# Causal attention in fp32: one score layout for all pairs of heads, whole loads of q and k, and fewer bytes moved

## Chip, cores and metric

One core of a Trainium2 chip. The metric is the device time of one execution in microseconds (us); a smaller time is better. The time is the median of several runs, beside one execution that the hardware profiler recorded.

## The reference

```python
scores = (q @ k.T) / sqrt(64), causal mask            # q, k, v: 4 batches x 12 heads x 448 x 64
attn   = softmax(scores);  x = attn @ v               # then x as 4 x 448 x 768
u = x + (relu(x.T @ w_tok1) @ w_tok2).T               # mixing of tokens, 448 -> 256 -> 448
x = u + relu(u @ w_ch1) @ w_ch2                       # feed-forward, 768 -> 1536 -> 768
theta = x @ w_theta
u = x + w_tok_r @ (x * cos(theta)) + w_tok_i @ (x * sin(theta))
out = u + relu(u @ w_ch)
```

All inputs are fp32 but the weights, which come as 64-bit numbers and are rounded on the chip.

## The kernel before, in words

The 48 heads (4 batches x 12) are worked in 24 pairs, numbered 0 to 23 (in words, pair one is number 0). A pair's two heads lie side by side along the free dimension: q and k are tiles of 64 partitions (the head dimension) by 896 columns. A pair's scores are made in seven tiles (`TILES`, line 326): tile 0 holds the first 64 query rows of both heads, tiles (i, h) with i = 1, 2, 3 hold 128 query rows of head h against 64 + 128 i keys. `scores` (line 338) makes a tile: the matmul (lines 358, 360), the masked maximum on VectorE (line 367), the exponential with its sum on ScalarE (line 369), and then the turning of the probabilities, so that `pv` (line 397) can multiply them with the values.

There are three kinds of pairs. Pairs 0 to 11 (`NATIVE`) multiply q and k as fp32; their tiles of q and k have 128 partitions of which the upper 64 are cleared by memset (line 281: VectorE for pair 0, POOL for pairs 1 to 11) while a DMA fills the lower 64 (line 286). Pairs 12 to 23 load q and k twice over, in both halves of the partitions (lines 288 and 290), and split them into a high and a low part (lines 297 to 302). Pairs 0 to 7 (`NATPV`) also multiply probabilities and values as fp32: every tile has a buffer of its own out of three, TensorE transposes it block by block (line 376, 1 + i blocks of 128 x 128, where the first block of a tile with i > 0 is half zeros: 64 cleared columns stand ahead of the buffer, line 257), ScalarE copies the blocks out of PSUM (line 378) into one of five buffers, and line 407 multiplies them with the values, 128 columns wide but for the last tile. Pairs 8 to 23 lay both heads of a tile side by side, the blocks of the first in reverse order, so that the two half blocks meet in the middle and make one; they split the probabilities into two fp16 parts (lines 387, 388), turn them by a DMA transpose on the SP queue (line 391), and multiply in three passes (lines 416, 424). Their values are split too, by ScalarE (line 124), POOL (line 163) and VectorE (line 323). The values have nine blocks of 64 columns.

The order of the work is written as 168 steps, one per tile (`steps`, line 620). Each step emits a tile's scores; `late_steps` (line 630) emits `pv` of the tile four steps earlier (five for pairs 8 to 23); at a pair's first step the loads of the next pair are emitted (line 695). Between these lie the rounding of the weights (`ROUNDINGS`, line 39: fetch on SP, line 173; ScalarE line 177, POOL line 130, VectorE lines 185 and 186; scaled split, POOL line 163 and VectorE line 197; store on SP, line 581) and, from step 53 on, the units of the feed-forward network (`UNIT_STEPS`): 24 units per batch, each of 18 fp16 matmuls of 448 columns (lines 231 to 233), whose weights `load_unit` (line 531) reloads from memory. The frame that builds the program then orders each engine's instructions by priorities and by its own estimate of times, so the order on an engine is not the order of the text; an engine works its list strictly in order. SP issues nearly all DMAs, so a wait on SP holds back all that stands behind it.

After the attention follow the remaining units, and the last layer (lines 724 on), which the change doesn't touch.

Of the kernel before, what the change touches and what calls it, by code (L numbers as in the profile page):

```python
# [18 lines left out]
P = 128  # L19
# [9 lines left out]
BUFS = dict(ut=12, h2=8, acc=12, ws=8, wf=3, raw=3, sb=3, pt=5, t=3, junk=1)  # L29
# [5 lines left out]
LATE_CONVERT = 16  # L35
FIRST_UNIT, DENSE, RATE = 53, 88, (42, 29)
# [18 lines left out]
def fused(ctx, tc, q, k, v, w_tok1, w_tok2, w_ch1, w_ch2, w_theta, w_tok, w_ch, out):  # L55
# [42 lines left out]
    def mm_bank():  # L98
        return bank("mm", 4)
# [154 lines left out]
    sb_all = ac.tile([P, BUFS["sb"] * 512], F32, tag="sb", name="sb")  # L254
    sbufs = [sb_all[:, j * 512:(j + 1) * 512] for j in range(BUFS["sb"])]
    for sb in sbufs:
        nc.gpsimd.memset(sb[:, 0:64], 0.0)
    pt_all = ac.tile([P, BUFS["pt"] * 512], F32, tag="pt", name="pt")
    ptfs = [pt_all[:, j * 512:(j + 1) * 512].rearrange("p (n q) -> p n q", q=P) for j in range(BUFS["pt"])]
    blocks = pt_all.bitcast(F16).rearrange("p (n q) -> p n q", q=P)  # L260
    count = [0]
# [14 lines left out]
    def prep(b, pr):  # L276
        qr = ap2.tile([P, 2 * S], F32, tag="qk_raw", name="q_raw", bufs=2)
        if b * NPR + pr in NATIVE:
            kr = ap2.tile([P, 2 * S], F32, tag="kh", name="k_pad")
            for t, src in ((kr, k), (qr, q)):  # L280
                (nc.vector if b * NPR + pr == 0 else nc.gpsimd).memset(t[64:128], 0.0)
                if b * NPR + pr == 0 and t is qr:
                    for c in (slice(0, 2 * P), slice(2 * P, 2 * S)):
                        nc.scalar.dma_start(out=t[0:64, c], in_=src[b, pr, 0:64, c])
                else:
                    loads[b * NPR + pr] = nc.sync.dma_start(out=t[0:64], in_=src[b, pr, 0:64])
        else:
            loads[b * NPR + pr] = nc.sync.dma_start(out=qr, in_=q[b, pr])
            kr = ap2.tile([P, 2 * S], F32, tag="qk_raw", name="k_raw", bufs=2)
            nc.sync.dma_start(out=kr, in_=k[b, pr])  # L290
        vr = ap2.tile([P, 9 * D], F32, tag="v_raw", name="v_raw")
# [3 lines left out]
        else:  # L295
            qs = ap2.tile([P, 2 * S], F32R, tag="qs", name="qs")
            copy_to(pick("qhi"), qs, qr)
            rest_to(pick("qlo"), qs[64:128], qr[64:128], qs[64:128])
# [15 lines left out]
    def value_split(n):  # L314
# [5 lines left out]
        hi = ap2.tile([P, 9 * D], F16, tag="v_hi", name="v_hi", bufs=2)  # L320
# [17 lines left out]
    def scores(pp, i, h):  # L338
# [6 lines left out]
        if pp.native_pv:  # L345
            cut = lambda t: t[:, h * S:h * S + n]
            if i == 0:
                cut = lambda t: t.rearrange("p (h s) -> p h s", h=2)[:, :, 0:64]
            msk = mask[:, S - kk:S]
        else:  # L350
            c0 = S if h == 1 else S - n + (64 + (n - kk) // 2 if i == 0 else 0)
            cut = lambda t: t[:, c0:c0 + n]
            if h == 0:
                src = ps[:, (n - kk) // (2 if i == 0 else 1):][:, 0:kk]
            msk = mask[:, S - kk:S] if h == 1 else mask[:, S - P:S - P + kk]
        if i == 0:
            msk = mask0.rearrange("p a b -> p (a b)")
        nc.tensor.matmul(ps[:, 0:n], lhsT=lhs, rhs=cut(pp.kh), start=True, stop=pp.kl is None)  # L358
        if pp.kl is not None:
            nc.tensor.matmul(ps[:, 0:n], lhsT=lhs, rhs=cut(pp.kl), start=False, stop=True)  # L360
        if pp.native_pv:
            full = sbufs[count[0] % BUFS["sb"]]
            sb = full[:, 64:64 + kk]
        else:
            both = (sb_all[:, 0:640], sb_all[:, 640:1536])[i % 2][:, 0:P if i == 0 else 2 * kk]
            sb = both[:, h * kk:(h + 1) * kk]
# [27 lines left out]
    def twice(ap):  # L394
        return ap.unsqueeze(1).to_broadcast([P, 2, D])
# [630 lines left out]
```

## Time and profile before

| | |
|---|---|
| median of 3 runs | 872.34 us (870.3 to 873.48) |
| the profiled execution | 871.68 us |
| its span, from the first to the last instruction | 869.9 us |
| mean granted TensorE clock | 0.998 of full speed |
| TensorE busy | 839.3 us (96%), 5699 matmuls |
| weight loads busy | 532.7 us (61%) |
| VectorE, ScalarE, POOL busy | 598.9, 531.3, 265.6 us |
| DMA | 151.99 MB |

PE is TensorE's matmul side, PEld its weight loads, DVE is VectorE, ACT is ScalarE, POOL is GpSimd, SP the engine that issues DMAs; a q behind a name (SPq) is the engine's sequencer. L376 is line 376 of the kernel. The ends of matmuls are modelled and they overlap, so a busy PE can still have room. A row of a group gives its count, its busy time in us and the mean duration in ns, and behind the bar the idle time of the engine before it, with what ended it.

### The profile page before, as it was taken

The numbers are of one execution on the slowest core, as the hardware profiler recorded it, in microseconds if no ns is written. First come the engines' busy times: TensorE is split into PE (matmuls) and PEld (weight loads), VectorE is DVE, ScalarE is ACT, GpSimd is POOL, SyncE is SP. The second block draws the span as 40 slices with busy tenths as digits, with TensorE's granted clock in tenths as the row PEclk, the third lists the DMA queues.
The fourth block names the chain that finished last, engine by engine and source line by source line (L and its number), as shares of the span: only waits on it lengthen the run. The fifth ranks groups of instructions, "written<-read, shape, count | busy, mean of one in ns | idle before, by whom it ended". The sixth has DMA issues, their size and how long they took to land.

```text
span 869.9 us, 16014 instructions
## 1 busy us (share of the span) xinstructions
PE 839.3 (96%) x5699; PEld 532.7 (61%) x5699; DVE 598.9 (69%) x1294; ACT 531.3 (61%) x1223; POOL 265.6 (31%) x445
## 2 busy tenths in 40 slices
PE   7999998899899999999999999999999999999997
PEld 6988856565657566576756655565555555555554
DVE  6788787999988556567774367669747548567541
ACT  6798786777767637367653276547647447456441
POOL 4366564547662220413222035331111001101000
PEclk9999999999999999999999999999999999999999
DMA  6866869999999976856475597702613123131012
GB/s 217 258 208 201 269 198 271 261 310 294 289 255 313 280 226 140 233 132 125 141 173 203 186 278 265 227 30 73 197 40 108 40 90 98 40 119 58 25 45 75
DMA packets 121024, 151.99 MB, mean 175 GB/s; under 512 B 76848, under 2 KB 88048, under 8 KB 120944
## 3 DMA queue, kind: packets, MB, share of 16 engines
q1 hardware_dynamic: 120400, 149.95, 59.4%
q0 software_dynamic: 384, 0.79, 0.4%
q8 instruction: 45, 0.74, 0.3%
q10 hardware_dynamic: 160, 0.23, 0.1%
q14 instruction: 35, 0.29, 0.1%
HBM read 110.56 MB, written 22.81 MB: 153 GB/s over the span
## 4 chain that ended last, share of the span: by engine, by line
PE 67%; DMA 10%; DVE 8%; ACT 5%; issue 5%; POOL 5%; SPq 0%; ACTq 0%; POOLq 0%; DVEq 0%
PE ps_mm L232 15%; PE ps_mm L231 15%; PE ps_mm L233 15%; DMA pt<-ph 5%; PE ps_sc L358 3%; PE ps_sc L231 3%; PE ps_sc L232 3%; PE ps_sc L233 3%; PE ps_pv L407 2%; DMA raw_w<-in_w_theta_dram 1%; PE ps_pv L424 1%; ACT junk L124 1%; ACT sb L369 1%; DVE sb L367 1%; PE ps_mm L376 1%
## 5 line engine op out<-in xcount | busy, mean ns | idle before, releaser
L231 PE MATMUL ps_mm<-h,ws 128*128 128x448 f16 x432 | 151.7, 354 | 1.6 <-DVE g L140 1.0
L232 PE MATMUL ps_mm<-h,ws 128*128 128x448 f16 x432 | 152.7, 354 | 0.1
L233 PE MATMUL ps_mm<-h,ws 128*128 128x448 f16 x432 | 152.5, 354 | 0.0
L231 PEld LDWEIGHTS <-ws 128*128 128x128 f16 x720 | 70.5, 98 | 67.2 <-issue 5.3
L233 PEld LDWEIGHTS <-ws 128*128 128x128 f16 x720 | 70.5, 98 | 63.9 <-issue 3.7
L232 PEld LDWEIGHTS <-ws 128*128 128x128 f16 x720 | 70.5, 98 | 62.5 <-issue 5.2
L369 ACT ACTIVATE sb<-sb,mx 128x320 f32<-128x320 f32 (+3 forms) x168 | 89.1, 533 | 25.6 <-DVE mx L367 25.0
L231 PE MATMUL ps_mm<-ut,ws 128*128 128x448 f16 x288 | 101.1, 353 | 1.4 <-DMA rawt<-x2d 1.3
L232 PE MATMUL ps_mm<-ut,ws 128*128 128x448 f16 x288 | 101.5, 353 | 0.8 <-DVE ut L197 0.8
L233 PE MATMUL ps_mm<-ut,ws 128*128 128x448 f16 x288 | 101.6, 353 | 0.0
L367 DVE CUSTOM_DVE_ANT_0 sb<-ps_sc,mask 128x320 f32<-128x320 f32 (+3 forms) x168 | 73.4, 455 | 17.7 <-PE ps_mm L376 11.3
L124 ACT ACTIVATE junk<-acc 128x448 bf16<-128x448 f32 x72 | 41.2, 572 | 59.1 <-DVE acc L912 41.3
L358 PE MATMUL ps_sc<-k_pad,q_raw 128*128 128x192 f32 (+3 forms) x168 | 56.9, 441 | 9.1 <-DMA k_pad<-in_k_dram 4.3
L787 POOL TENSOR_SCALAR tmp<-tmp 128x384 f32<-128x384 f32 x28 | 15.6, 556 | 148.6 <-ACT tmp L786 145.6
L388 DVE SCALAR_TENSOR_TENSOR ph<-sb,ph 128x128 f16<-128x128 f32 (+1 forms) x64 | 46.8, 736 | 19.0 <-ACT ph L160 18.3
L163 POOL TENSOR_SCALAR h<-t 128x448 f16<-128x448 f32 x48 | 35.2, 735 | 75.7 <-ACT t L497 75.2
L497 ACT ACTIVATE t<-ps_mm,c_scale 128x448 f32<-128x448 f32 x48 | 30.0, 625 | 41.3 <-PE ps_mm L233 36.2
L160 ACT ACTIVATE ph<-sb 128x128 f16<-128x128 f32 (+1 forms) x64 | 39.6, 625 | 25.6 <-DMA pt<-ph 25.3
L499 DVE TENSOR_TENSOR h<-t,h 128x448 f16<-128x448 f32 x48 | 32.0, 670 | 27.0 <-POOL h L163 26.9
L130 POOL TENSOR_SCALAR raw<-raw 128x768 f32<-128x768 f32 (+2 forms) x34 | 35.4, 1041 | 41.6 <-ACT wf L177 37.0
L231 PE MATMUL ps_sc<-th,ut 128*128 128x384 f16 x144 | 46.9, 326 | 0.0
L233 PE MATMUL ps_sc<-th,ut 128*128 128x384 f16 x144 | 46.8, 326 | 0.0
(218 smaller groups left out, 2119.4 us busy)
## 6 DMA issues: line engine op xcount, KB each, us to landing
ws<-w_c SPq DMA_DIRECT2D x120, 384.0 KB, 4.6
raw<-in_w_ch_dram SPq DMA_DIRECT2D x30, 768.0 KB, 5.6
w_c<-ws SPq DMA_DIRECT2D x30, 384.0 KB, 4.3
v_raw<-in_v_dram SPq DMA_DIRECT2D x24, 288.0 KB, 4.9
q_raw<-in_q_dram SPq DMA_DIRECT2D x12, 448.0 KB, 4.2
k_raw<-in_k_dram SPq DMA_DIRECT2D x12, 448.0 KB, 5.4
x2d<-acc SPq DMA_DIRECT2D x24, 224.0 KB, 3.8
acc<-x2d SPq DMA_DIRECT2D x24, 224.0 KB, 2.6
```

The source lines that it names most:

```text
L124: nc.scalar.activation(j[:, 0:src.shape[-1]], src, AF.Square, accum_out=dst)
L130: nc.gpsimd.tensor_scalar(out=dst, in0=a, scalar1=b, scalar2=c, op0=ALU.mult, op1=ALU.mult)
L160: nc.scalar.activation(dst, src, AF.Copy, scale=scale)
L163: e.tensor_scalar(out=dst, in0=src, scalar1=scale, scalar2=0.0, op0=ALU.mult, op1=ALU.add)
L231: nc.tensor.matmul(ps, lhsT=ka(a[:, 0]), rhs=kb(b[:, 0]), start=first, stop=False)
L232: nc.tensor.matmul(ps, lhsT=ka(a[:, 0]), rhs=kb(b[:, 1]), start=False, stop=False)
L233: return nc.tensor.matmul(ps, lhsT=ka(a[:, 1]), rhs=kb(b[:, 0]), start=False, stop=last)
L358: nc.tensor.matmul(ps[:, 0:n], lhsT=lhs, rhs=cut(pp.kh), start=True, stop=pp.kl is None)
L367: pp.first = nc.vector.tensor_tensor_reduce(out=sb, in0=src, in1=msk, op0=ALU.add, op1=ALU.min, scale=-0.125, scalar=3.0e38, accum_out=pp. ...
L369: pp.last = nc.scalar.activation(sb, sb, AF.Exp, bias=pp.mx[:, j:j + 1], scale=-1.0, accum_out=pp.sm[:, 2 + j:3 + j])
L388: nc.vector.scalar_tensor_tensor(out=lo, in0=both, scalar=PSC, in1=hi, op0=ALU.mult, op1=ALU.subtract)
L499: gates[0] = nc.vector.tensor_tensor(out=t[:, 1], in0=f, in1=t[:, 0], op=ALU.subtract)
```

## The change

Pairs 0 to 7 take the layout that pairs 8 to 23 had: both heads of a tile side by side, transposed together (at most four blocks to a PSUM bank) and copied to fixed places, in fp32. Transposes of tiles i = 1, 2, 3 then need 3, 5 and 7 blocks for both heads; `pv` runs for both heads at the second one, and only the first head's products are 128 columns wide. q of pairs 0 to 11 moves to the buffers of `qs`, so that `qk_raw` is left to pairs 12 to 23. k and q of pairs 1 to 9 come as 128 partitions from memory, where q has zeros in the upper 64, and need no memset. q of pairs 12 to 23 is loaded into 64 partitions only and split across them. The ninth block of the values goes; tile 0 uses blocks 6 and 7. Weight tiles of units 20 to 23 stay in place after their store and are not reloaded.

```diff
...
-BUFS = dict(ut=12, h2=8, acc=12, ws=8, wf=3, raw=3, sb=3, pt=5, t=3, junk=1)
+BUFS = dict(ut=12, h2=8, acc=12, ws=8, wf=3, raw=3, t=3, junk=1)
...
+WHOLE = 10
+FIRST_DIRECT = 20
...
-    sb_all = ac.tile([P, BUFS["sb"] * 512], F32, tag="sb", name="sb")
...
+    sb_all = ac.tile([P, 1536], F32, tag="sb", name="sb")
+    pt_all = ac.tile([P, 2560], F32, tag="pt", name="pt")
+    blocks32 = pt_all.rearrange("p (n q) -> p n q", q=P)
+    blocks16 = pt_all.bitcast(F16).rearrange("p (n q) -> p n q", q=P)
...
     def prep(b, pr):
-        qr = ap2.tile([P, 2 * S], F32, tag="qk_raw", name="q_raw", bufs=2)
-        if b * NPR + pr in NATIVE:
+        n = b * NPR + pr
+        if n in NATIVE:
+            qr = ap2.tile([P, 2 * S], F32, tag="qs", name="q_raw")
             kr = ap2.tile([P, 2 * S], F32, tag="kh", name="k_pad")
...
+            if n == 0:
+                nc.vector.memset(kr[64:128], 0.0)
+                loads[n] = nc.sync.dma_start(out=kr[0:64], in_=k[b, pr, 0:64])
+                nc.vector.memset(qr[64:128], 0.0)
+                for c in (slice(0, 2 * P), slice(2 * P, 2 * S)):
+                    nc.scalar.dma_start(out=qr[0:64, c], in_=q[b, pr, 0:64, c])
+            elif n < WHOLE:
+                nc.sync.dma_start(out=kr, in_=k[b, pr])
+                loads[n] = nc.sync.dma_start(out=qr, in_=q[b, pr])
+            else:
+                for t, src in ((kr, k), (qr, q)):
+                    nc.gpsimd.memset(t[64:128], 0.0)
+                    loads[n] = nc.sync.dma_start(out=t[0:64], in_=src[b, pr, 0:64])
         else:
-            loads[b * NPR + pr] = nc.sync.dma_start(out=qr, in_=q[b, pr])
-            kr = ap2.tile([P, 2 * S], F32, tag="qk_raw", name="k_raw", bufs=2)
+            qr, kr = (ap2.tile([P, 2 * S], F32, tag="qk_raw", name=f"{x}_raw", bufs=2) for x in "qk")
+            loads[n] = nc.sync.dma_start(out=qr[0:64], in_=q[b, pr, 0:64])
             nc.sync.dma_start(out=kr, in_=k[b, pr])
-        vr = ap2.tile([P, 9 * D], F32, tag="v_raw", name="v_raw")
+        vr = ap2.tile([P, 8 * D], F32, tag="v_raw", name="v_raw")
         nc.sync.dma_start(out=vr, in_=v[b, pr])
...
-            copy_to(pick("qhi"), qs, qr)
-            rest_to(pick("qlo"), qs[64:128], qr[64:128], qs[64:128])
+            copy_to(pick("qhi"), qs[0:64], qr[0:64])
+            rest_to(pick("qlo"), qs[64:128], qr[0:64], qs[0:64])
...
-        hi = ap2.tile([P, 9 * D], F16, tag="v_hi", name="v_hi", bufs=2)
+        hi = ap2.tile([P, 8 * D], F16, tag="v_hi", name="v_hi", bufs=2)
...
+        c0 = S if h == 1 else S - n + (64 + (n - kk) // 2 if i == 0 else 0)
+        cut = lambda t: t[:, c0:c0 + n]
+        if h == 0:
+            src = ps[:, (n - kk) // (2 if i == 0 else 1):][:, 0:kk]
         if i == 0:
             msk = mask0.rearrange("p a b -> p (a b)")
+        else:
+            msk = mask[:, S - kk:S] if h == 1 else mask[:, S - P:S - P + kk]
...
+        both = (sb_all[:, 0:640], sb_all[:, 640:1536])[i % 2][:, 0:P if i == 0 else 2 * kk]
+        sb = both[:, h * kk:(h + 1) * kk]
...
         if i > 0 and h == 0:
             return
         m = both.shape[-1]
+        first = {3: 26, 2: 16, 1: (10, 0)[pp.pr % 2], 0: (8, 6)[pp.pr % 2]}[i]
+        if pp.native_pv:
+            pt = pp.pts[i] = blocks32[:, first // 2:first // 2 + m // P]
+            for u0 in range(0, m // P, 4):
+                pst = mm_bank()
+                nt = min(4, m // P - u0)
+                for u in range(nt):
+                    nc.tensor.transpose(pst[:, u * P:(u + 1) * P], both[:, (u0 + u) * P:(u0 + u + 1) * P], ident)
+                nc.scalar.activation(pt[:, u0:u0 + nt].rearrange("p n q -> p (n q)"), pst[:, 0:nt * P], AF.Copy)
+            return
...
     def pv(pp, i, h):
         if pp.ps is None:
             pp.ps = bank("pv", 1)
...
         if i > 0 and h == 0:
             return
...
+        pt, nb = pp.pts[i], 2 * i + 1
+        parts = ((0, 0),) if pp.native_pv else ((0, 0), (0, 1), (1, 0))
+        for h in range(2 if i > 0 else 1):
+            reg = (2 * i + h) * D
+            n = 2 * D if i == 0 or (pp.native_pv and h == 0) else D
+            if i == 0:
+                jobs = [(0, 6)]
+            else:
+                jobs = [(i, 6 + h)] + [(i + 1 + u if h else i - 1 - u, 2 * u + h) for u in range(i)]
+            for j, (blk, vt) in enumerate(jobs):
+                for m, (half, c) in enumerate(parts):
+                    pp.pv = nc.tensor.matmul(pp.ps[:, reg:reg + n], lhsT=pt[:, half * nb + blk], rhs=pp.v[c][:, vt * D:vt * D + n],
+                                             start=j + m == 0, stop=j == len(jobs) - 1 and m == len(parts) - 1)
...
     def round_store(j):
         n = ROUNDINGS[j][1]
         if n >= 0:
-            nc.sync.dma_start(out=jobs[n][1], in_=rounding.pop(j))
+            w = rounding.pop(j)
+            nc.sync.dma_start(out=jobs[n][1], in_=w)
             stored.add(n)
+            if n >= FIRST_DIRECT:
+                loaded[n] = w
...
-    native = np.array([n in NATPV for n in range(B * NPR)]).reshape(B, NPR, 1, 1)
...
+        whole = np.array([n < WHOLE for n in range(B * NPR)]).reshape(B, NPR, 1, 1)
+        return c(np.concatenate([t, np.where(whole, np.zeros_like(t), t)], axis=2))
...
-    for x, y in ((a0, np.where(native, a0, zero)), (np.where(native, b0, zero), b0), (a0, b0)):
+    for x, y in ((a0, zero), (zero, b0)):
```

## Rows read from the trace of the kernel before

**Rows 1.** Busy time of each engine, share of the span and instructions (the page).

```profile
PE 839.3 (96%) x5699; PEld 532.7 (61%) x5699; DVE 598.9 (69%) x1294; ACT 531.3 (61%) x1223; POOL 265.6 (31%) x445
```

**Rows 2.** Timeline of PE at 128 us: start, us, line, tiles, form.

```profile
128.07 0.35 PE L232 MATMUL ps_mm<-ut,ws 128*128 128x448 f16 x1
128.26 0.35 PE L233 MATMUL ps_mm<-ut,ws 128*128 128x448 f16 x1
```

**Rows 3.** Windows: stretch, length, busy PE, PEld, DVE, ACT, POOL, clock, DMA share, GB/s.

```profile
0.00:121.00 121.00, 111.97 (x775) 94.75 (x776) 95.19 (x257) 96.77 (x265) 67.64 (x110) 1.00 0.71 224
...
75.00:100.00 25.00, 23.90 (x169) 20.52 (x169) 20.88 (x49) 19.48 (x56) 15.40 (x21) 1.00 0.82 258
...
121.00:180.00 59.00, 53.74 (x401) 34.53 (x401) 51.39 (x114) 39.76 (x99) 32.54 (x45) 0.97 1.05 264
180.00:300.00 120.00, 112.63 (x915) 74.94 (x915) 105.66 (x237) 86.16 (x210) 57.01 (x82) 1.00 1.04 293
```

**Rows 4.** A group of PE by form, then PE's timeline, runs of one form merged.

```profile
L376 PE MATMUL ps_mm<-ident,sb 128*128 128x128 f32 x152 | 24.3, 277 | 0.0
...
12.03 0.61 PE L407 MATMUL ps_pv<-v_raw,pt 128*128 128x128 f32 x4
...
19.72 0.55 PE L407 MATMUL ps_pv<-v_raw,pt 128*128 128x64 f32 x4
...
21.31 0.72 PE L376 MATMUL ps_mm<-ident,sb 128*128 128x128 f32 x5
```

**Rows 5.** Chain of waits: start, us, what; the pieces on line 281.

```profile
49.19 0.85 POOL q_raw L281
...
105.43 0.84 POOL k_pad L281
106.27 0.79 POOL q_raw L281
```

**Rows 6.** Groups of ACT by form, first 121 us: copies out of PSUM.

```profile
L378 ACT ACTIVATE pt<-ps_mm 128x512 f32<-128x512 f32 x16 | 9.5, 597 | 6.1 <-PE ps_mm L376 6.0
...
L378 ACT ACTIVATE pt<-ps_mm 128x256 f32<-128x256 f32 x16 | 6.0, 377 | 0.4 <-PE ps_mm L376 0.3
```

**Rows 7.** Waits, first 121 us: who for whom, us, times, longest.

```profile
PEld ps_pv L407 <- ACT pt L378: 2.0, 2, 1.2
...
PE ps_pv L407 <- ACT pt L378: 0.8, 2, 0.6
```

**Rows 8.** Tile v_hi: durations in ns, least, median, most; who waited.

```profile
L163 POOL TENSOR_SCALAR v_hi<-v_raw,sv x16: 742/749/1902, 112.6 to 460.2; 128x576 f16<-128x576 f32 x16
...
  PE ps_pv L416: 2.1, 2
```

**Rows 9.** DMA issues of q and k: count, KB each, median us to landing.

```profile
k_raw<-in_k_dram SPq DMA_DIRECT2D x12, 448.0 KB, 5.4
...
k_pad<-in_k_dram SPq DMA_DIRECT2D x12, 224.0 KB, 5.3
q_raw<-in_q_dram SPq DMA_DIRECT2D x11, 224.0 KB, 6.0
```

**Rows 10.** Waits for weight reloads, 225 to 300 us.

```profile
SPq L226 <- DMA w_c<-ws: 5.5, 1, 5.5
...
PEld L231 <- DMA ws<-w_c: 1.0, 1, 1.0
...
PE ps_mm L231 <- DMA ws<-w_c: 0.6, 1, 0.6
```

**Rows 11.** The stretch at 160 us: windows, then PE's timeline.

```profile
160.00:164.00 4.00, 1.41 (x19) 1.02 (x15) 4.00 (x10) 3.53 (x8) 1.72 (x3) 0.99 1.02 341
164.00:168.00 4.00, 4.00 (x15) 1.86 (x13) 4.00 (x11) 3.15 (x7) 1.18 (x3) 0.58 1.38 256
...
164.53 0.58 PE L231 MATMUL ps_mm<-h,ws 128*128 128x448 f16 x1
164.90 0.58 PE L232 MATMUL ps_mm<-h,ws 128*128 128x448 f16 x1
```

More of the change, by code (lines that the diff above doesn't have):

```diff
@@ L252, in fused @@
     wt2 = ac.tile([P, 2, 2, S], F32R, tag="wt2", name="wt2")
-    sb_all = ac.tile([P, BUFS["sb"] * 512], F32, tag="sb", name="sb")
[L255 to L261, printed above, removed]
+    sb_all = ac.tile([P, 1536], F32, tag="sb", name="sb")
+    pt_all = ac.tile([P, 2560], F32, tag="pt", name="pt")
+    blocks32 = pt_all.rearrange("p (n q) -> p n q", q=P)
+    blocks16 = pt_all.bitcast(F16).rearrange("p (n q) -> p n q", q=P)
     def tok_weights(n):
@@ L360, in scores @@
             nc.tensor.matmul(ps[:, 0:n], lhsT=lhs, rhs=cut(pp.kl), start=False, stop=True)
[L361 to L366, printed above, removed]
+        both = (sb_all[:, 0:640], sb_all[:, 640:1536])[i % 2][:, 0:P if i == 0 else 2 * kk]
+        sb = both[:, h * kk:(h + 1) * kk]
         pp.first = nc.vector.tensor_tensor_reduce(out=sb, in0=src, in1=msk, op0=ALU.add, op1=ALU.min, scale=-0.125,
@@ L370, in scores @@
                              accum_out=pp.sm[:, 2 + j:3 + j])
-        if pp.native_pv:
-            nt = 1 + i
-            c0 = 64 if i == 0 else 0
-            pst = mm_bank()
-            for u in range(nt):
-                nc.tensor.transpose(pst[:, u * P:(u + 1) * P], full[:, c0 + u * P:c0 + (u + 1) * P], ident)
-            pt = ptfs[count[0] % BUFS["pt"]]
-            nc.scalar.activation(pt[:, 0:nt].rearrange("p n q -> p (n q)"), pst[:, 0:nt * P], AF.Copy)
-            pp.pts[i, h] = pt
-            count[0] += 1
-            return
         if i > 0 and h == 0:
@@ L388, in scores @@
         nc.vector.scalar_tensor_tensor(out=lo, in0=both, scalar=PSC, in1=hi, op0=ALU.mult, op1=ALU.subtract)
-        first = {3: 26, 2: 16, 1: (10, 0)[pp.pr % 2], 0: (8, 6)[pp.pr % 2]}[i]
-        pt = blocks[:, first:first + m // 64]
+        pt = blocks16[:, first:first + m // 64]
         pp.sent = nc.sync.dma_start_transpose(out=pt, in_=ph[:, 0:2 * m])
         pp.pts[i] = pt
-    def twice(ap):
-        return ap.unsqueeze(1).to_broadcast([P, 2, D])
     def pv(pp, i, h):
@@ L970, in pairs @@
         else:
-            back = np.concatenate([t[..., 0, r] for r in rows[::-1]] + [t[..., 1, :]], axis=3)
-            t = np.where(native, t.reshape(B, NPR, D, 2 * S), back)
+            t = np.concatenate([t[..., 0, r] for r in rows[::-1]] + [t[..., 1, :]], axis=3)
         t = t.reshape(B, NPR, D, 2 * S)
-        return c(np.concatenate([t, t], axis=2))
+        if not tails_first:
+            return c(np.concatenate([t, t], axis=2))
+        whole = np.array([n < WHOLE for n in range(B * NPR)]).reshape(B, NPR, 1, 1)
+        return c(np.concatenate([t, np.where(whole, np.zeros_like(t), t)], axis=2))
     v = inputs["v"].reshape(B, NPR, 2, S, D)
```

42 lines of the change are left out of this document (removed).

## The prediction

> **What bounds the kernel now.** I read the busy times of the page first [rows 1]. TensorE is busy 839.3 of 869.9 us, weight loads 532.7, VectorE 598.9, ScalarE 531.3. A busy TensorE need not be full, since matmuls overlap, so the second look is at their spacing [rows 2]: matmuls of 448 columns last 0.35 us each, but one starts every 0.19 us, in unbroken runs. Where that spacing holds, only fewer instructions on TensorE shorten the kernel. The third look is at the stages [rows 3]. Of its 30.6 idle us (869.9 - 839.3) TensorE has 21.7 before 300 us (9.0, 5.3 and 7.4 in three stages) and 8.9 in the 570 us behind. Before 300 us VectorE is busy 79 to 88% and ScalarE 67 to 80%, so they are close behind. The change works almost wholly before 300 us, so it can win in two ways: instructions taken off TensorE, which count in full, and waits shortened, of which there are at most some 20 us. The profiled execution took 871.7 us, 0.7 below the median of 872.3; the sum below is made against 871.7.
>
> **The change, part by part.**
>
> Transposes. In each of pairs 0 to 7 the seven score tiles were transposed one by one, 1+4+6+8 = 19 blocks; side by side, tiles i = 1, 2, 3 need 3, 5 and 7 blocks and tile 0 one, 16 in all. That removes 24 of 152. A transpose lasts 277 ns, but five in a row end 0.72 us after the first starts [rows 4], so they are (0.72 - 0.28) / 4 = 0.11 us apart. 24 x 0.11 = 2.7 us, off TensorE in full. The Trainium skill (TensorE: Matmul & The Clock Gate, Part 4: PE-mode transpose) gives about 275 ns for one transpose in a kernel. By that price the sum would fall by 6.6 us; the rows agree with the length and not with the spacing, and I go by the spacing.
>
> Value products. Their number stays; in tiles 1 and 2 the second head's five products per pair shrink from 128 to 64 columns, two passes each: 5 x 2 x 8 = 80 passes. Four passes of 128 columns take 0.61 us from first start to last end, four of 64 take 0.55 [rows 4]: over three spacings that is 0.02 us apart at most, and less by what the last pass itself is shorter. The gain lies between nothing and 80 x 0.02 = 1.6 us; I take 0.6, under the middle for that last pass.
>
> Clearings. 18 memsets of 0.84 us leave POOL, 15 us. They cost time only where POOL is what the others wait for. The chain of waits runs through three of them [rows 5]: one at 49.2 us, and two in a row at 105.4 us, behind the rounding of weights and ahead of scale factors. Together they hold 0.85 + 0.84 + 0.79 = 2.5 us of the chain, the upper bound; the lower is nothing, if ScalarE or VectorE is as late. I take half, 1.2. The others are counted as nothing: POOL is busy 68 of the first 121 us [rows 3], and its gaps cover them. Should POOL be short in more places, the gain grows.
>
> Copies out of PSUM. ScalarE made seven per pair with 128 + 2 x (256 + 384 + 512) = 2432 columns. It now makes six, of 128, 384, 512 + 128 and 512 + 384, 2048 in all. By the copies of 512 and 256 columns, 0.597 and 0.377 us [rows 6], a column costs 0.86 ns and a copy 0.16 us besides. So a pair saves 384 x 0.86 ns + 0.16 = 0.49 us, eight pairs 3.9 us of ScalarE, hidden mostly by TensorE's own work; 0.4 taken, bounds 0 and 3.9.
>
> Grouping. Blocks of a tile's first head now wait for the second head's exponentials, and their products follow together. What is queued behind a late group on TensorE is the next score tile. The nearest rows are TensorE's waits for a copy, 0.8 and 2.0 us in four waits [rows 7]. I charge 0.5, bounds 0 and 2.8. The score buffers do the opposite: three in turn become two by parity. Only the next pair's first head of tile 1 finds its buffer held by a tile that is nearer (tile 3, which ends two steps earlier instead of three); the others keep or gain distance. I count nothing for it.
>
> Values. 512 columns for 576 shorten the split of the values on POOL, 0.75 us, by a ninth in 16 pairs [rows 8]. TensorE waited for it 2.1 us in two waits. I take 0.3; bounds 0 and 16 x 0.08 = 1.3.
>
> Loads. q and k of pairs 1 to 9 double in bytes, q of pairs 12 to 23 halves. I count both as nothing, by the landings [rows 9]: loads of 224 KB into 64 partitions took 5.3 (k) and 6.0 us (q) in the median, the load of 448 KB into 128 partitions (k) 5.4. A half load is no quicker than a whole one. The Trainium skill (SBUF — State Buffer, Door 1: The DMA port swizzle) says why: partitions 0 to 63 reach 8 of the 16 ports. By that rule the halved q gains nothing either, which speaks against that part of the change. The trace agrees as far as these three medians go. The cover of the whole loads is time: one issued in one pair is needed in the next. At the start the values of pair 0 queue behind them; bounds for the delay are 0 and 448 KB at the 224 GB/s of that stretch [rows 3], 2 us, for work that is not yet due: 0 taken. That q no longer shares buffers with the raw q and k of pair 12 frees their load; TensorE runs the feed-forward units meanwhile, and I count nothing.
>
> Reloads. Units 20 to 23 take their weights from the tile that was stored, so four loads of 384 KB go. TensorE waited for such a load once for 0.6 and its weight queue once for 1.0 us, and the SP queue stood 5.5 us on the store that a reload had to await, with all that follows on SP behind it [rows 10]. I take 0.7; bounds 0 and 1.6.
>
> Sum: -2.7 - 0.6 - 1.2 - 0.4 + 0.5 - 0.3 - 0.7 = -5.4, so 871.7 - 5.4 = **866.3 us**, 6.0 or 0.7% under the median.
>
> **The rivals.**
>
> The waits take it back (24 in 100). TensorE sheds 3.3 us, but no chain before 300 us gets shorter, because VectorE, ScalarE and POOL replace one another as the last to end, and the grouping costs its full 2.8. 871.7 - 3.3 + 2.8 = 871.2 us, no change. For it: VectorE at 79% and more in each of those stages [rows 3]. Against it: ScalarE and POOL both lose work.
>
> The bytes count after all (10 in 100), the case on the other side. The place is the SP queue, where the raw weights for rounding queue behind k and q of the next pair. If whole loads cost by their bytes, each pair adds 448 KB, 1.8 us at the 258 GB/s that the busiest stretch before 121 us reached [rows 3], and the rounding, which feeds the units, falls back by that much in each of the nine pairs: 866.3 + 9 x 1.8 = 882.5 us. It decides once the DMA engines are full; their share there is 0.71 to 0.82, against 1.04 and 1.05 in the later stages. Against it stand the landings.
>
> The hole at 160 us (14 in 100). TensorE idles 2.6 of the 4 us from 160 us on, with VectorE at work without a pause, and in the next 4 us the granted clock has a mean of 0.58, so it stood at the 1.2 GHz level for most of them [rows 11]. Matmuls then started 0.37 instead of 0.19 us apart; by the mean clock those 4 us lost 4 x 0.42 = 1.7. Such a hole costs 4.3 us. The order of instructions is laid anew, so this one may close, 862.0 us (7 in 100), or a second may open, 870.6 (7 in 100).
>
> That the change does not do what it says I see only for the halved q, which is in the forecast as nothing.
>
> **How the numbers follow.** The forecast has the remaining 52 in 100. A measurement of this kernel can tell some 0.5% (4.4 us) from no change. Faster by more: forecast and closed hole, 0.59. Within: waits that take it back and a second hole, 0.31. Slower: the bytes, 0.10. The range goes from 860 (all gains but ScalarE's at their bounds, 2.7 + 1.6 + 2.5 + 0.4 + 1.3 + 1.6 = 10.1, thus 861.6, and a little below for a closed hole) to 873 (871.2 and the 1.6 by which the runs before scattered to either side); it leaves out the bytes and the edges of the others.
>
> **What would show it.** Transposes x128 in place of 152, and copies x48 in place of 56, of the same lengths by size. No memset of q and k but four on POOL, and POOL some 15 us less busy. Idle TensorE before 121 us at about 6 instead of 9 us; before 300 us all stages together some 6 us shorter. The whole k and q loads landing within 6 us of issue; if they take 8 us or more and ScalarE's conversion of raw weights waits for them, the bytes count. Four reloads fewer and no wait of SP on their stores. The forecast is wrong if TensorE's waits for copies grow beyond 3 us, or if a stretch of lower clock appears at another place.

## The result and the profile after

The changed kernel takes 878.44 us in the median of six runs (877.0 to 879.4) against 871.93 us of the kernel before in six runs (870.0 to 874.2): ratio 1.0078, 95% interval 1.006 to 1.0095. It is **slower by 6.5 us** where 5.4 us less were forecast. Its profiled execution took 878.4 us with a span of 876.6; the one before 871.7 and 869.9. Two runs at a low mean granted clock, one of `b_wm` (1442 us, 0.558) and one of the kernel before (962.6 us, 0.851), are left out of all medians, means and ratios below.

The busy line of the page, which answers to [rows 1]:

```profile
PE 841.9 (96%) x5675; PEld 534.3 (61%) x5675; DVE 598.3 (68%) x1294; ACT 527.3 (60%) x1215; POOL 247.3 (28%) x424
```

The work has shrunk as foreseen: 24 fewer matmuls, 8 fewer copies, 18 us less of POOL. Yet TensorE shows more busy time. In stretches of low clock a matmul lasts longer: 0.53 to 0.58 us instead of 0.35, as the lines under `a_hold8` show. Next the stages, same columns as [rows 3]:

```profile
0.00:121.00 121.00, 109.93 (x737) 92.25 (x737) 95.24 (x259) 94.76 (x260) 56.93 (x89) 0.97 0.76 262
...
121.00:180.00 59.00, 52.11 (x413) 33.72 (x413) 47.83 (x107) 37.73 (x91) 26.73 (x39) 0.97 0.98 245
180.00:300.00 120.00, 112.77 (x887) 76.49 (x886) 103.68 (x227) 82.83 (x201) 58.03 (x82) 0.96 0.97 258
```

TensorE idles 11.1 us in the first stage (9.0 before), not the 6 that the forecast named, and its clock is below 1.00 in all three (0.97 stood in the second before the change too). The DMA share has fallen in the later two, so the transfers are not fuller than before. Where the loss arises is read from the stores of the first batch's results, six per batch; the two lines are of the kernel before (first and last start of the six), then of the changed one:

```profile
L520 SPq DMA_DIRECT2D x2d<-acc x6: 319/348/948, 260.8 to 280.7; - x6
```

```profile
L500 SPq DMA_DIRECT2D x2d<-acc x6: 327/382/780, 267.4 to 286.3; - x6
```

The sixth leaves 5.6 us late. The last store of all left 6.4 us late (616.4 and 622.8 us), and the whole span is 6.7 us longer: nearly all of it is lost **before 287 us**. The attention of the first eight pairs, where the change takes work away, was ahead: the last output of a pair that the trace has before 122 us (line 435, now 415) started at 102.1 us against 103.7.

Four stretches of low clock stand in windows of 4 us (columns as above), where the profile of before had only the one at 164 us [rows 11]. That one is gone:

```profile
108.00:112.00 4.00, 1.43 (x12) 1.14 (x13) 2.50 (x6) 4.00 (x10) 3.90 (x7) 1.00 0.90 322
112.00:116.00 4.00, 2.80 (x7) 1.31 (x7) 3.40 (x9) 2.86 (x9) 1.02 (x1) 0.57 0.41 146
116.00:120.00 4.00, 4.00 (x16) 2.79 (x15) 4.00 (x12) 2.14 (x5) 2.49 (x4) 0.58 0.00 0
156.00:160.00 4.00, 3.55 (x28) 2.22 (x29) 3.14 (x10) 3.28 (x9) 0.89 (x1) 0.61 0.78 238
...
216.00:220.00 4.00, 4.00 (x46) 3.04 (x44) 4.00 (x7) 4.00 (x10) 4.00 (x6) 0.71 1.00 365
232.00:236.00 4.00, 3.51 (x13) 3.27 (x13) 4.00 (x14) 2.58 (x9) 2.90 (x7) 0.50 1.05 283
```

The first follows a stretch in which TensorE was busy 1.43 of 4 us. It waited there for the first feed-forward unit's input, the split tile ut of the first batch (104 to 122 us; us in total, times, longest):

```profile
PE ps_mm L234 <- DVE ut L199: 2.2, 2, 1.5
PE ps_mm L233 <- ACT ut L162: 1.5, 1, 1.5
```

Between 121 and 300 us the waits of TensorE were these in the kernel before, by size from the fifth on down,

```profile
PE ps_sc L358 <- DVE mx L367: 1.3, 2, 1.0
PE ps_pv L424 <- DMA pt<-ph: 1.1, 2, 0.8
```

and in the changed one these lead:

```profile
PE ps_sc L358 <- DVE mx L363: 5.6, 6, 1.8
PE ps_pv L404 <- DMA pt<-ph: 4.5, 2, 3.2
```

Both waits belong to pairs nine and later, whose layout of scores the change leaves alone; what differs there are loads, clearings and the blocks of the values. VectorE, whose busy time in all is the same (598.9 and 598.3 us), got less of it done in those 179 us, 151.5 against 157.1 us (before, then after; columns as in [rows 3]):

```profile
121.00:300.00 179.00, 166.37 (x1314) 109.48 (x1314) 157.06 (x350) 125.92 (x307) 89.55 (x127) 0.99 1.04 283
```

```profile
121.00:300.00 179.00, 164.87 (x1298) 110.21 (x1298) 151.51 (x332) 120.56 (x291) 84.76 (x121) 0.96 0.97 254
```

Those 5.5 us are about what the first batch is late. So the first theory was this. **The parts do what they were priced at, and the instructions, laid out anew on every engine, stand in a worse order**: TensorE waits longer and its clock falls. The rivals: one part is to blame (whole loads, side-by-side, the tiles used directly), by bytes or by waits of its own.

How far an order has moved is counted by laying two programs' lists of TensorE's matmuls side by side, where a matmul is known by the names, types and shapes of its operands: those outside the longest sequence that both lists share have moved. The changed kernel shares 4928 of 5439 with the kernel before. The counts in the expectations are larger (82 for a 42, some 900 for a 387). A matching of common blocks comes near to them, and it misses entries that both lists share; the text goes by the longest sequence.

### The profile page after: what moved, and what is told of

Same layout as the page of the kernel before. It is cut to its first block, busy times and chain, and to the rows that moved or that the text cites. A ratio compares the mean times of both kernels' runs of the same rounds, so it can differ in the third digit from the quotient of the medians.

```text
span 876.6 us, 15888 instructions
## 1 busy us (share of the span) xinstructions
PE 841.9 (96%) x5675; PEld 534.3 (61%) x5675; DVE 598.3 (68%) x1294; ACT 527.3 (60%) x1215; POOL 247.3 (28%) x424
## 4 chain that ended last, share of the span: by engine, by line
PE 63%; DVE 11%; DMA 9%; ACT 6%; POOL 5%; issue 5%; SPq 0%; DVEq 0%; ACTq 0%; POOLq 0%
PE ps_mm L235 16%; PE ps_mm L234 16%; PE ps_mm L233 16%; DMA pt<-ph 5%; PE ps_sc L358 3%; PE ps_pv L404 2%; PE ps_sc L235 2%; PE ps_sc L234 2%; PE ps_sc L233 2%; DMA ws<-w_c 2%; ACT sb L365 2%; DVE wf L187 1%; POOL raw L132 1%; DVE wf L188 1%; DVE ph L383 1%
## 5 line engine op out<-in xcount | busy, mean ns | idle before, releaser
L234 PE MATMUL ps_mm<-ut,ws 128*128 128x448 f16 x288 | 102.1, 355 | 2.3 <-DVE ut L199 2.2
L404 PE MATMUL ps_pv<-v_raw,pt 128*128 128x64 f16 (+3 forms) x608 | 71.6, 235 | 0.2 <-DVE v_raw L328 0.2
L358 PE MATMUL ps_sc<-k_pad,q_raw 128*128 128x192 f32 (+3 forms) x168 | 58.7, 459 | 6.6 <-DMA k_pad<-in_k_dram 4.7
L165 POOL TENSOR_SCALAR h<-t 128x448 f16<-128x448 f32 x48 | 31.9, 666 | 67.5 <-ACT t L477 63.1
L132 POOL TENSOR_SCALAR raw<-raw 128x768 f32<-128x768 f32 (+2 forms) x34 | 34.7, 1021 | 44.5 <-ACT wf L179 40.8
L233 PE MATMUL ps_sc<-th,ut 128*128 128x384 f16 x144 | 46.9, 326 | 0.0
```

The source lines that it names most:

```text
L132: nc.gpsimd.tensor_scalar(out=dst, in0=a, scalar1=b, scalar2=c, op0=ALU.mult, op1=ALU.mult)
L233: nc.tensor.matmul(ps, lhsT=ka(a[:, 0]), rhs=kb(b[:, 0]), start=first, stop=False)
L234: nc.tensor.matmul(ps, lhsT=ka(a[:, 0]), rhs=kb(b[:, 1]), start=False, stop=False)
L404: pp.pv = nc.tensor.matmul(pp.ps[:, reg:reg + n], lhsT=pt[:, half * nb + blk], rhs=pp.v[c][:, vt * D:vt * D + n], start=j + m == 0, stop=j ...
```

## The experiments

Times are medians; each ratio is to the kernel before, run beside it, with its 95% interval. Each profile is of one execution.

**Which part? One undone or one alone.**

```
u_direct:   FIRST_DIRECT = 20  ->  99
u_whole:    WHOLE = 10  ->  1
side_alone: both of these, and q whole, nine value blocks, q in its former buffers
b_whole:    before: for pairs two to ten, in place of clearing and half load
            loads[...] = nc.sync.dma_start(out=t, in_=src[b, pr])
```

> The changed kernel with one part undone: the last four weight tiles are stored and read back again, as before the change. The theory of the holes (the priced gains came, and new idle stretches of TensorE, each followed by a half clock, took them and more) expects what the changed kernel gave, 876 to 880 us, with the stretches of lower clock near 112, 156, 212 and 232 us still there, since the direct tiles enter only from the 21st unit on. The rival that the four tiles, held longer in the ring of eight, are what delays the units expects 871 to 874 us and a clock of 1.00 from 180 us on.

878.94 us, 1.0083 (1.0053 to 1.0113): no part of the loss, and no gain either from the reloads saved. Its profile kept the low clock at 112 us and had none at 156, 212 and 232, where the expectation had them stay, but one at 172 us.

> The changed kernel with the whole loads undone: q and k of pairs two to ten are half loads again, with the clearings on GpSimd. The theory of the holes expects 876 to 880 us if side-by-side is where the holes come from. The rival that the whole loads (4 MB more on the queues before 121 us) are to blame, by bytes or because they take GpSimd's clearings away and so let the first units come earlier than their inputs, expects 870 to 874 us, and no half clock at 112 us.

879.78 us, 1.0094 (1.0057 to 1.013), low clock at 112 us included. Undoing the whole loads gives nothing back.

> The changed kernel with everything undone but the two heads side by side in the first eight pairs (half loads with clearings, whole q, nine value blocks, reloads, q in its former buffers). If side-by-side opens the holes: 875 to 880 us, with the holes of the changed kernel. If side-by-side gives what it was priced at (2.7 of transposes, 0.6 of value products, 0.4 of copies, less 0.5): 868 to 870 us, and the loss lies in another part.

882.78 us, 1.0132 (1.0105 to 1.0159), worse than all parts together.

> The kernel before with one part of the change: q and k of pairs two to ten whole, without clearings. Priced at a gain of 1.2 us, so 869 to 872 us, if whole loads land as half loads do. If the whole loads are to blame (bytes, or GpSimd set free too early): 875 us or more. The theory of the holes allows either, but ties the time to the stretches: each new one at half clock is worth 1.7 to 2 us of clock and the wait that stands ahead of it.

878.58 us, 1.009 (1.0062 to 1.0119). So two parts that share no line lose 7 and 11 us when each stands alone, and 6.5 together. Costs of the parts would add; a cost of *any* move of the order need not. In b_whole 339 of 5439 matmuls have moved, in side_alone 457.

**The bytes and the order, apart.**

```
b_wm:      before: as b_whole, but
           (nc.vector if ... else nc.gpsimd).memset(t[64:128], 0.0)   stays ahead of the load
b_first54: before: FIRST_UNIT, DENSE, RATE = 53 -> 54, 88, (42, 29)
b_first52: before: FIRST_UNIT, DENSE, RATE = 53 -> 52, 88, (42, 29)
```

> The kernel before, with q and k of pairs two to ten loaded whole, but the clearings kept (each is overwritten by its load): the same 4 MB more on the queues as in b_whole, while GpSimd does what it did and the instructions of TensorE keep their order but for 14 of 5441. If the bytes or the landing of whole loads cost the 7 us that b_whole lost, this gives 876 to 880 us. If what cost them is the other order of the instructions that goes with the clearings, this gives 870 to 874 us, as the kernel before.

871.0 us, 0.9999 (0.998 to 1.0019). The same whole loads, in nearly the same order, cost nothing that these runs can tell (the interval allows 2 us). The bytes are out as the cause of the 7 us.

> The kernel before with the first unit asked for at step 54 instead of 53: no work is added or taken, some 900 of TensorE's 5441 matmuls stand elsewhere. If the order by itself is worth what the change lost (the kernel before has a lucky one), this gives 875 to 882 us, with other stretches at half clock than the one at 164 us. If the parts of the change are to blame and not the order, 870 to 874 us.

882.32 us, 1.0111 (1.0068 to 1.0153): **11 us lost by a kernel that does the same work as before**. The first batch's last store leaves at 290.8 us, and between 121 and 300 us the same two waits have grown (then two of its windows with low clock):

```profile
PE ps_sc L358 <- DVE mx L367: 7.0, 5, 2.4
PE ps_pv L424 <- DMA pt<-ph: 4.1, 5, 1.7
```

```profile
136.00:140.00 4.00, 2.79 (x19) 2.25 (x20) 2.41 (x10) 2.75 (x9) 0.38 (x1) 0.63 1.11 408
244.00:248.00 4.00, 2.51 (x9) 1.16 (x9) 4.00 (x11) 2.67 (x7) 1.56 (x3) 0.78 1.11 275
```

> The kernel before with the first unit asked for at step 52 instead of 53: the same work, some 670 of TensorE's 5441 matmuls stand elsewhere. If the order of the kernel before is one of the best of many near it, this loses as the later one did: 875 to 883 us. If 54 only lost because the units came later, the earlier one gives 868 to 873 us.

880.59 us, 1.0084 (1.0059 to 1.0109). Earlier loses as later does. The two edits move 276 (b_first52) and 387 (b_first54) matmuls.

**Is it the grouping, or the hole at 108 us?**

```
side_split: side_alone, but per head
            lo, hi = (0, 1) if i == 0 else ((0, i), (i, 2 * i + 1))[h]
            transposes and copy of blocks lo to hi; products of the first head's
            own blocks behind the first head
a_hold8:    after, in the first unit, ahead of its products
            for _ in range(8): nc.tensor.matmul(ps[:, 0:S], lhsT=w[:, 0, 0:P],
                                   rhs=uT[0][:, 0], start=True, stop=True)
```

> Side-by-side alone (as side_alone), but with the transposes, their copy and the products of each step in two parts again, one behind each head's exponential, as before the change. If it is the coarser work (one block of up to seven transposes and ten products behind both heads) that leaves TensorE with nothing to put into the wait for the first unit's input at 108 to 115 us, this gives back 4 to 8 of the 11 us that side_alone lost: 874 to 878 us, and a clock of 1.00 between 100 and 121 us. If the order in general is to blame, it stays within 878 to 884 us.

883.3 us, 1.0126 (1.0094 to 1.0157). The hole at 108 us did close, with 3.90 of 4 us busy against 2.43 in side_alone; four us later TensorE still idles 1.7 us:

```profile
108.00:112.00 4.00, 3.90 (x32) 3.36 (x30) 1.82 (x10) 4.00 (x11) 3.73 (x11) 1.00 1.02 398
112.00:116.00 4.00, 2.26 (x13) 1.25 (x12) 4.00 (x11) 4.00 (x10) 2.46 (x5) 1.00 0.48 187
```

The clock is 1.00 there (0.68 and 0.50 from 112 us on in side_alone), and nothing came back at the end. The clock did what the theory of the coarser work expected and the time did not: this hole is not where the loss is decided, and the grouping is not the cause of the loss.

> The changed kernel, with the first product of the first unit done nine times instead of once (each starts its sum anew, so that what is computed is the same): 8 matmuls of 0.19 us more, that fall into the wait of 108 to 113 us. If the half clock from 112 to 119 us comes from that wait, it goes or shortens: 2 to 3.5 us less for the lost clock, at most 1.5 us more for the matmuls, so 874 to 878 us. If the clock there comes from something else, the clock stays half and the time is 878 to 881 us.

876.19 us, 1.0047 (1.0025 to 1.0069), 2.3 us less than the changed kernel: within the expectation, though the two intervals overlap. TensorE's timeline from the wait on, first of the changed kernel, then with the eight more (one line has all of them):

```profile
109.79 0.35 PE L233 MATMUL ps_mm<-ut,ws 128*128 128x448 f16 x1 [1.53 <-ACT ut L162]
...
112.51 0.53 PE L234 MATMUL ps_mm<-ut,ws 128*128 128x448 f16 x1 [1.54 <-DVE ut L199]
112.84 0.58 PE L235 MATMUL ps_mm<-ut,ws 128*128 128x448 f16 x1
```

```profile
109.81 1.67 PE L477 MATMUL ps_mm<-ut,ws 128*128 128x448 f16 x8 [1.55 <-ACT ut L163]
...
112.51 0.35 PE L235 MATMUL ps_mm<-ut,ws 128*128 128x448 f16 x1
112.69 0.35 PE L236 MATMUL ps_mm<-ut,ws 128*128 128x448 f16 x1
```

The second product starts at 112.51 us in both: the eight cost nothing in place. From there on matmuls are 0.19 us apart instead of 0.33 to 0.37, and no window of 4 us before 300 us has a low clock. In these two executions the half clock at 112 us goes with the wait, and with the wait filled it is gone. A wait of this size does not always bring it: in the profile of a_dvemid (below) TensorE is as idle there, with no matmuls added, and the clock stays at 1.00:

```profile
108.00:110.00 2.00, 0.42 (x5) 0.30 (x4) 1.33 (x4) 2.00 (x7) 1.84 (x4) 1.00 0.99 370
110.00:112.00 2.00, 1.43 (x12) 1.11 (x12) 1.56 (x2) 2.00 (x5) 2.00 (x5) 1.00 1.00 403
112.00:114.00 2.00, 0.46 (x4) 0.17 (x2) 1.50 (x3) 2.00 (x6) 0.47 (x1) 1.00 0.33 131
```

What the filled wait is worth in time is less sure. The profiled execution of a_hold8, with its full clock, took 879.3 us, the slowest of its ten and no less than the changed kernel's 878.4; and the eight matmuls also moved 262 others, where orders of the changed kernel with no work changed differ by 2.1 us (next). At most it is the smaller part of the loss.

**Do the changed kernel's own neighbours scatter?**

```
a_first54, a_first52: after: FIRST_UNIT 53 -> 54, 52
a_dense90:            after: DENSE 88 -> 90
```

> The changed kernel with the first unit asked for at step 54: the same work, some 380 of 5417 matmuls stand elsewhere. If the loss is one of order, the times of the changed kernel's own neighbours scatter as those of the kernel before do, by 3 to 10 us, and some lie below 873; this one anywhere from 868 to 884. If the loss sits in what the change does, all of them give 876 to 881 us.

880.51 us, 1.0099 (1.0078 to 1.0119).

> The changed kernel with the first unit asked for at step 52: some 820 of 5417 matmuls stand elsewhere. As for a_first54: by the theory of the order anywhere from 868 to 884 us, by a loss that sits in the parts 876 to 881 us.

879.86 us, 1.0084 (1.0062 to 1.0105).

> The changed kernel with its first fourteen units spread up to step 90 instead of 88: some 1100 of 5417 matmuls stand elsewhere. As for a_first54: by the theory of the order anywhere from 868 to 884 us, by a loss that sits in the parts 876 to 881 us.

879.37 us, 1.0078 (1.0056 to 1.01). None is below 873, and all four orders of the changed kernel (878.4 among them) lie within 2.1 us of one another, the three new ones with 175, 261 and 490 matmuls moved. The theory of the order expected a scatter of 3 to 10 us and some times below 873; here the rival that the loss sits in the parts has its numbers right. Yet the two neighbours of the kernel before, without any part of the change, lie at 880.6 and 882.3. Like against like, with the first unit asked for at the same step, the change makes next to no difference:

| first unit at step | without the change | with it |
|---|---|---|
| 52 | 880.6 (1.0084) | 879.9 (1.0084) |
| 53 | 871.9 | 878.4 (1.0078) |
| 54 | 882.3 (1.0111) | 880.5 (1.0099) |

What stands out is not the changed kernel but the one order of the kernel before.

**What sets the pace, and where?** In three kernels work is left out, in a fourth a buffer is doubled. All four also move 220 to 360 matmuls against the changed kernel, so some 2 us of their differences can be the order's.

```
a_pvless: value products of pairs one to eight, only the first block of each head
          ... for u in range(0 if pp.native_pv else i)]
a_pvmid:  parts = ((0, 0),) if pp.b * NPR + pp.pr < 15 else ((0, 0), (0, 1), (1, 0))
          and units 0 to 5 without the third product of mm3
a_dvemid: second instruction of round64 only where ROUNDINGS[j][0] < 50
a_ph20:   ph: bufs=1 -> (2, 1)[i % 2]; the tails' transpose by two matmuls with ident
```

> The changed kernel with 96 of the value products of the first eight pairs left out (only the first block of each head is multiplied): 10.6 us less for TensorE (96 by 0.11), all before 121 us, where the change itself saves its 3.7. If TensorE's work there sets the time, 866 to 870 us. If its savings there are swallowed by the first unit's wait for its input from ScalarE and VectorE at 108 to 113 us, the first transposed block of pair nine (119.13 us in the changed kernel, 119.29 in the one before) leaves less than 4 us earlier, and the time is 873 to 880 us.

868.72 us, 0.9977 (0.9957 to 0.9997): 9.7 us less than the changed kernel. The first transposing transfer of pair nine left at 110.5 us (119.1 in the changed kernel), so what was gained arrived. But the work taken was not 10.6 us. The expectation counts 96 products at 0.11 us, and an fp32 product is two passes in the trace, so 192 passes went (the changed kernel, then a_pvless):

```profile
L404 PE MATMUL ps_pv<-v_raw,pt 128*128 128x128 f32 x160 | 24.1, 281 | 0.0
L404 PE MATMUL ps_pv<-v_raw,pt 128*128 128x64 f32 x144 | 19.7, 264 | 0.0
```

```profile
L404 PE MATMUL ps_pv<-v_raw,pt 128*128 128x128 f32 x64 | 13.0, 288 | 0.7 <-DVE x L415 0.4 <-ACT pt L378 0.3
L404 PE MATMUL ps_pv<-v_raw,pt 128*128 128x64 f32 x48 | 8.2, 254 | 0.0
```

In the changed kernel ten such passes take 1.22 us from first start to last end, so they are (1.22 - 0.28) / 9 = 0.104 us apart:

```profile
43.13 1.22 PE L404 MATMUL ps_pv<-v_raw,pt 128*128 128x128 f32 x10
```

192 of them are 20 us, and TensorE's busy time fell by as much, from 841.9 to 822.2 us. So **before 121 us, too, only about half of the work taken from TensorE came back**: 9.7 of 20. That the time fell into the range 866 to 870 us is luck of the wrong price.

> The changed kernel with 302 matmuls left out between 121 and 300 us: two of the three value products of pairs nine to fifteen (266 by 0.029 us) and the third product of the first six units (36 by 0.19): 14.5 us less for TensorE, nothing less for any other engine. If TensorE sets the pace of that stretch, 863 to 867 us. If VectorE, ScalarE and the transfers do, with TensorE waiting more instead, 872 to 878 us.

872.1 us, 1.0004 (0.9988 to 1.002): 6.3 us for 14.5. Its mean granted clock over ten runs is 0.985, against 0.9905 of the changed kernel; so some of what is missing may have gone to the lower clock.

> The changed kernel with 13 instructions of VectorE left out between 110 and 300 us (the second half of the rounding of 64-bit weights, 1.04 us each: the last three bits of those weights are dropped): 13.5 us less for VectorE, nothing less for any other engine. If VectorE's work sets the pace of that stretch, 865 to 870 us; if TensorE alone does, 876 to 881 us.

872.88 us, 1.0012 (0.9992 to 1.0032): 5.6 us for 13.5. Both stretches, 121 to 300 us (a_pvmid, then a_dvemid):

```profile
121.00:300.00 179.00, 157.46 (x1012) 101.59 (x1011) 154.07 (x341) 122.28 (x297) 85.98 (x124) 0.94 0.98 254
```

```profile
121.00:300.00 179.00, 164.13 (x1314) 107.63 (x1313) 143.74 (x336) 122.75 (x302) 82.69 (x127) 0.99 0.98 259
```

Relieving either engine returns some 40% of what was taken. Neither paces that stretch alone. That the two hand work to each other, and that an order decides how well the hand-overs fit, is the likely reading; no run shows it by itself.

> The changed kernel with two buffers instead of one for the scaled blocks (ph) of the even steps that the transposing transfers read; room is made by computing the tails' transpose in two matmuls, 2.6 us more of TensorE in all (24 by 0.11). ScalarE waited 21.7 us for these buffers between 121 and 300 us (15.5 before the change). If that wait sets the pace, it halves and the time is 868 to 875 us. If not, 877 to 884 us.

881.93 us, 1.0112 (1.0073 to 1.0151). ScalarE's wait for the buffer fell from 21.7 us to less than half (the changed kernel, then a_ph20),

```profile
ACT ph L162 <- DMA pt<-ph: 21.7, 13, 4.6
ACT sb L365 <- DVE mx L363: 7.2, 9, 1.8
```

```profile
ACT sb L365 <- DVE mx L363: 18.9, 10, 7.0
ACT ph L162 <- DMA pt<-ph: 9.5, 5, 3.5
```

and the time was put in elsewhere: ScalarE now waits 18.9 us for VectorE's maxima. Here again fp32 products were priced at one pass: the 24 more are 48 passes, some 5 us, and TensorE's busy time rose by 5.6. Even with all of that taken off, 877 us are left, and 868 to 875 were expected of a buffer that sets the pace. The single buffer is not the knot.

**Does the cost grow with what moves?**

```
b_direct: before: w = rounding.pop(j); ...; if n >= 20: loaded[n] = w
b_qd:     b_direct, and q of pairs 13 on: dma_start(out=qr[0:64], in_=q[b, pr, 0:64]),
          qhi and qlo from qr[0:64]
```

> The kernel before with one part of the change, the last four weight tiles used without storing and reading back first: 82 of TensorE's 5441 matmuls stand elsewhere, all behind the 1600th. Priced at 0.7 us: 870 to 872 us if the order counts by how much of it moves; 876 to 882 us if any other order than that of the kernel before loses 8 us.

874.83 us, 1.005 (1.0031 to 1.007): between the two expectations, and so in neither.

> As b_direct, and with q of pairs thirteen on loaded in half, copied from half the rows (two parts of the change together): 207 of 5441 matmuls stand elsewhere. By the sum 870 to 872 us; 872 to 875 us if the loss grows with what moves (14 moved cost nothing, 670 to 910 cost 7 to 11 us); 876 to 882 us if any other order loses 8 us.

877.23 us, 1.0069 (1.0047 to 1.0091). That is in the range of "any other order loses 8 us", and above the 872 to 875 us of a loss that grows with what moves. With the runs above, all edits of the kernel before:

| kernel | matmuls moved, of 5439 | us | against before |
|---|---|---|---|
| b_wm | 13 | 871.0 | 0.9999 |
| b_direct | 42 | 874.8 | 1.005 |
| b_qd | 141 | 877.2 | 1.007 |
| b_first52 | 276 | 880.6 | 1.008 |
| b_whole | 339 | 878.6 | 1.009 |
| b_first54 | 387 | 882.3 | 1.011 |
| side_alone | 457 | 882.8 | 1.013 |

The loss grows with what moves, steeply at first and then slowly, over edits of several kinds (b_qd contains b_direct), two of which change no work at all. That the order of the kernel before is worth some 8 to 11 us against its neighbours is shown by b_first52 and b_first54. Around the changed kernel moving costs little: its 175, 261 and 490 moved matmuls went with 2.1, 1.4 and 0.9 us. So it is no price per moved matmul, but what leaving that one order costs. Which hand-over makes it so good was not found.

**The clock over many runs.** Each run lists its mean granted clock. Over 75 runs of the kernel before, those beside the experiments, it has a mean of 0.9950, so 0.0050 x 869 = 4.4 us were lost to it; the profiled execution (0.998) was a fortunate one. Over six runs of the changed kernel the mean is 0.9905, 8.3 us lost. Within the 75 runs, a microsecond lost to the clock goes with 0.58 us of time (correlation 0.63). By that price, an estimate, the 3.9 us more of the changed kernel are worth 2.3 us; a_hold8, with a mean of 0.9949 over ten runs, was 2.3 us faster. The price is rough: within the seven other kernels with eight runs or more it lies between 0.01 and 0.52. That would leave 4.2 of the 6.5 us to waits. TensorE's idle time in the two profiles grew by 4.1 us, 34.7 (876.6 - 841.9) against 30.6, but these two executions lie further apart in clock (0.988 and 0.998) than the means do.

## Why the prediction was wrong

**The step that failed** is the case of the hole at 160 us: "The order of instructions is laid anew, so this one may close, 862.0 us (7 in 100), or a second may open, 870.6 us (7 in 100)." The prediction saw that the order changes, and priced that by the one hole that the trace showed, as if a new order could differ by one such hole to either side; the sum itself has nothing for it. The runs show another size and another centre: same work in another order took 8 to 11 us more, in both directions of the shift. The order of before was not an average draw, so the change of order was no term around nothing but one of about +8 to +11.

**A second step failed under it**: "instructions taken off TensorE, which count in full". In a_pvless 20 us of TensorE's work before 121 us gave 9.7 us, in a_pvmid 14.5 us behind it gave 6.3. By that half, the 3.3 us of transposes and value products would have been worth some 1.6 us at best (an estimate).

Of the sum itself little is seen. With the first unit at step 52 and at 54, the changed kernel is 0.7 and 1.8 us faster than the kernel before at the same step, by the ratios 0.0 and 0.1%, within the intervals. So the gain of 5.4 us was not there, nor does the change cost anything beside the order that it gives up. This rests on two pairs of kernels.

Point by point:

- *Transposes, value products, copies.* The counts came as forecast, 128 transposes and 48 copies:

```profile
L377 PE MATMUL ps_mm<-ident,sb x128: 272/273/421, 7.6 to 110.7; 128*128 128x128 f32 x128
```

Of their 3.3 us the changed kernel was ahead by 1.6 at 102 us and by 0.2 at 119 us, where pair nine's first transfer leaves at 119.1 (119.3 before). Between the two lie the wait for the first unit's input and the half clock behind it. How much each took is not separated.
- *"Where that spacing holds, only fewer instructions on TensorE shorten the kernel."* The spacing does not hold throughout before 300 us, and fewer instructions of VectorE shortened the kernel too: 13.5 us less gave 5.6 (a_dvemid).
- *Clearings.* Four of 0.84 us are left on POOL, two of each:

```profile
L290 POOL MEMSET k_pad<- 64x896 f32 x2 | 1.7, 840 | 0.1
L290 POOL MEMSET q_raw<- 64x896 f32 x2 | 1.7, 840 | 0.0
```

POOL is 18.3 us less busy. The 1.2 us were not seen: u_whole, which brings the clearings back, differs by less than the intervals.
- *Grouping.* TensorE's weight queue waited for a copy 0.5 us in two waits before 121 us, TensorE itself not at all, far from the bound of 2.8 us, and side_split, which takes the grouping back, gained nothing. Its 0.5 was right or too much.
- *Loads as nothing.* Right. Whole loads landed in 4.8 (k) and 5.5 us (q), against 5.3 and 6.0 of the half ones [rows 9], and b_wm gives 0.9999:

```profile
k_pad<-in_k_dram SPq DMA_DIRECT2D x9, 448.0 KB, 4.8
q_raw<-in_q_dram SPq DMA_DIRECT2D x9, 448.0 KB, 5.5
q_raw<-in_q_dram SPq DMA_DIRECT2D x14, 224.0 KB, 5.6
```

The prediction left out one row of the kernel before, the whole loads of q of pairs 12 to 23, which landed faster than the half ones:

```profile
q_raw<-in_q_dram SPq DMA_DIRECT2D x12, 448.0 KB, 4.2
```

Halved, they are 12 of the 14 that landed in 5.6 us. So the rival of the bytes falls, although it had the right sign of the time. The rule of the Trainium skill that was weighed there (SBUF — State Buffer, Door 1: The DMA port swizzle), by which half the partitions reach half the ports, agrees with these landings.
- *Reloads.* 116 for 120, but u_direct (878.9) and the changed kernel (878.4) are the same within their intervals. The 0.7 us are not seen.
- *The waits take it back* had the right idea, engines that replace one another, and kept its harm at 2.8 us, since it let only the grouping add waits.
- *What would make it wrong*: "a stretch of lower clock appears at another place." It did, in four. As a sign it was right; as a cause it carries about a third of the loss by the estimate above (2.3 of 6.5 us).

Side-by-side in the order of the kernel before was not tried, since the order follows from the lengths of the instructions themselves. No kernel that computes the whole result was found that beats the kernel before; of those with the change, a_hold8 is the fastest at 876.2.

## What to carry to other kernels

Where an order of instructions is laid out anew with every edit, and the kernel before may have been chosen by its time (here no run shows how it was), take the order itself as a term: run two edits that change no work (a start one step earlier, one later) before pricing a gain below 1%, and put the changed kernel against them at the same settings, not against the one best order alone. An edit worth less than what neighbouring orders differ by has to be followed by a new choice of the order, or be made so that nothing moves. In this kernel TensorE and VectorE were busy 92 and 85% of the stretch from 121 to 300 us, and work taken from either counted by less than half there; from TensorE in the stretch before, by about half. And count what the trace counts: an fp32 product was two passes, so a price per pass has to be taken twice.

## What the runs showed of the hardware that was not expected

- With eight matmuls put into a wait, the granted clock was 1.00 in the following 8 us (0.57 and 0.58 without them), and they cost no time in place. In another kernel (a_dvemid) it stayed at 1.00 behind a like wait without them.
- The mean granted clock of one and the same kernel differs from run to run, 0.990 to 1.000 over 75 runs, and in them a microsecond lost to it goes with 0.58 us of time.
- Taking 192 fp32 passes, 20 us of TensorE's time, out of a stretch where TensorE was busy 91% shortened the kernel by 9.7 us.
- Halving ScalarE's wait for a buffer (21.7 to 9.5 us) made the kernel no faster, at some 5 us more of TensorE's work; ScalarE's wait for VectorE grew by 11.7 us.
